# Attention and two gated layers on one core: a second handoff time in the planner, output products held four parts behind, and one attention's due times moved

## The chip, the cores and the metric

The kernel runs on one core of a Trainium2 chip. The metric is the device time of one execution in microseconds (us), the median over several executions. The engines are TensorE (PE in the profile; its weight loads are PEld), VectorE (DVE), ScalarE (ACT), GpSimd (POOL) and SyncE (SP), which issues all the transfers here.

## The reference

Everything is float32. The reference is three steps in a row over 4608 tokens of 512 features:

```python
scores = scale * (q_c @ k_c.T)            # chunks of 64 tokens, 8 heads of 64
attn = exp(scores - max) / (sum + 1e-9)
x = (attn @ v_c)                          # -> 4608 x 512
g = x @ w_gate                            # first layer, 512 -> 1536 -> 512
x = (g * sigmoid(g) * (x @ w_val)) @ w_out
h = x @ w_in                              # second layer, 512 -> 2048 -> 512
out = (h * sigmoid(1.702 * h)) @ w_out2
```

## The kernel before, in words

**Tiling.** The tokens are cut into nine blocks of 512. The first layer's 12 feature tiles are done in two passes over all blocks (six tiles a pass, three groups of two), the second layer's 16 in two more passes (eight tiles a pass, two groups of four). So pass 0 and 1 are the first layer, pass 2 and 3 the second, and a second-layer pass has nine blocks of two groups. Sums between the two passes of a layer go through DRAM (`y_dram`, `o_dram`). The last pass adds the kept sum and writes `out`.

**Products.** Every matrix product is done as seven half-size products (labels 1 to 7) with sums of quarters before and after, and every operand is split into a high and a low part, so that one product is 12 matmuls of 256 columns (`mm3`, L247 to L250: high by high, high by low, low by high). A second-layer group has seven input products (`product`, L567) and then 14 output parts (`last_product`, L713: two for each of seven labels, six matmuls each).

**The shared bank.** In `group_gated` (L631) the seven input products of a group are written into one PSUM bank, `ga`, one after the other in the order 1, 6, 7, 5, 2, 4, 3 (only the very first second-layer group gives three of them banks of their own). Each product must wait until the previous one's reader has read the bank. These readers stand in `follow` (L659): an ACT copy for labels 1, 6, 7 and 5, and a DVE addition for 2, 4 and 3. Behind the readers comes the chain that makes the operands of the output parts: a sigmoid on ACT and a product on DVE (`gate`, L646), sums on DVE, and the split into a high part (a cast on ACT) and a low part (a subtraction on DVE or POOL) in `parts` (L655). While a reader runs, TensorE does output parts of an earlier group.

**The order.** No engine's order is written out by hand. Every operation is recorded with an engine, an estimated duration, a priority (a due time; the lower comes first) and its dependencies; `Program.emit` (L99) then walks a model of the engines: it takes on each engine the operation that could start first, and of those that could start within 0.3 us of it (0.1 us on DVE) the one of the lowest priority. This order is the order of the engine's queue, which is processed in order on the chip. The model's time from the end of one operation to the start of one that needs it is `late`: 0.3 us between engines, 1.2 us into TensorE, 1.5 us more after a transfer, 0.13 us on the same engine. The input products of the second layer are marked `near` and get 0.25 us. The model has no contention between engines.

**Due times.** In the main loop (L864 on) the output parts of a group wait in a list, `pend`. After each of the next group's seven products, `put` takes some of them off the list, records them, and gives them the due time of that point; in the second layer two after each product, until none is left after the seventh. The order of the labels is 1, 2, 4, 5, 6, 7, 3. `o_sum` (L731), called with the second part of a label in a block's second group, adds the outputs up: in the last pass it loads the sum of the earlier pass (`part_of`), adds to it on POOL and DVE, and stores to `out` (`out_quarter`).

**The start.** In pass 0 the attention of the next block (four calls of `attend`, L463, of 128 tokens each) is recorded with each block. Each has loads of q, k and v (issued by SP, due 10 us ahead), two sets of 32 small matmuls and a transposition on TensorE, six DVE operations (L487 to L495), an exponential and two copies on ACT. `x_made` (L538) then makes the seven input operands of the block (sums on DVE, casts on ACT, subtractions on POOL). Next to this the first layer's weights are unpacked and split on ACT, DVE and POOL (`conv_part`, `split`).

Of the kernel before, what the change touches and what calls it, by code (L numbers as in the profile page):

```python
# [69 lines left out]
class Program:  # L70


    def __init__(self):
        self.ops = []

    def op(self, eng, us, fn, reads=(), writes=(), prio=0, table=None, near=False):
        o = Op()
        o.eng, o.us, o.fn, o.prio, o.table, o.near, o.n = eng, us, fn, prio, table, near, len(self.ops)
        deps, follows = set(), set()
        for b in reads:  # L80
            deps.update(next((a.writers for a in b.line() if a.writers), ()))
        for b in writes:
            deps.update(b.users)
            if not b.users:
                if b.prev is not None:
                    deps.update(b.prev.users)
                if b.before is not None and b.before.tile is None:
                    follows.add(b.before.users[0])
        for b in (*reads, *writes):
            for a in b.line():  # L90
                a.users.append(o)
        for b in writes:
            for a in b.line():
                a.writers.append(o)
        o.deps, o.follows = deps, follows - deps
        self.ops.append(o)
        return o

    def emit(self):  # L99
        waiting = {o: len(o.deps) + len(o.follows) for o in self.ops}  # L100
        after = {}
        for o in self.ops:
            for d in (*o.deps, *o.follows):
                after.setdefault(d, []).append(o)
        ready = {}
        for o in self.ops:
            o.done_at = 0.0
            if not waiting[o]:
                ready.setdefault(o.eng, []).append(o)
        free, table = {}, None  # L110
        left = len(self.ops)
        while left:
            pick = None
            for eng, todo in ready.items():
                if not todo:
                    continue
                t = free.get(eng, 0.0)
                start = [max(t, o.done_at) for o in todo]
                first = min(start)
                s, o = min(((s, o) for s, o in zip(start, todo) if s <= first + (0.1 if eng == "dve" else 0.3)), key=lambda x: (x[1].prio, x[1].n))  # L120
                if pick is None or s < pick[0]:
                    pick = s, o
            s, o = pick
            ready[o.eng].remove(o)
            free[o.eng] = s + o.us + (1.3 if o.table and o.table != table else 0.0)
            end = free[o.eng] + (2.0 if o.eng == "dma" else 0.0)
            table = o.table or table
            o.fn()
            left -= 1
            for a in after.get(o, ()):  # L130
                if o in a.deps:
                    late = (0.3, 1.2)[a.eng == "pe" and o.eng != "pe"] + (1.5 if o.eng == "dma" else 0.0)
                    if a.near and o.eng != "dma":
                        late = 0.25
                    a.done_at = max(a.done_at, end + ((0.0 if a.eng == "pe" else 0.13) if a.eng == o.eng else late))
                waiting[a] -= 1
                if not waiting[a]:
                    ready.setdefault(a.eng, []).append(a)
# [3 lines left out]
def attention_two_moe_kernel(ctx: ExitStack, tc: tile.TileContext, q, k, v, wg, wv, wo, wi, wo2, out):  # L142
# [38 lines left out]
    UPB = BT // P  # L181
    EARLY = 8
    FILL = 24
    scale = 1.0 / float(D) ** 0.5

    pool = {}
# [25 lines left out]
    def act_us(n):  # L212
        return (200 + n) / 1.2e3
# [13 lines left out]
    def store(dst, src, writes, prio):  # L227
        op("dma", 0.74 / 512 * size(dst), lambda: nc.sync.dma_start(out=dst, in_=bits(src.ap)), [src], writes, prio)

    def copy(dst, src, n, prio, eng="act", cut=lambda ap: ap):  # L230
        if eng == "act":
            op("act", act_us(n), lambda: nc.scalar.copy(out=dst.ap, in_=cut(src.ap)), [src], [dst], prio)  # L232
        elif eng == "pool":
            op("pool", pool_us(0.6 * n), lambda: nc.gpsimd.tensor_copy(dst.ap, cut(src.ap)), [src], [dst], prio)  # L234
        else:
            op("dve", dve_us(n), lambda: nc.vector.tensor_copy(dst.ap, cut(src.ap)), [src], [dst], prio)

    def tt(dst, a, b, by, n, prio, eng="dve", of_a=lambda ap: ap, of_b=lambda ap: ap):
        e = nc.vector if eng == "dve" else nc.gpsimd
        op(eng, dve_us(n) if eng == "dve" else pool_us(n),  # L240
           lambda: e.tensor_tensor(out=dst.ap, in0=of_a(a.ap), in1=of_b(b.ap), op=by), [a, b], [dst], prio)  # L241

    def split(hi, lo, src, n, prio, eng="dve", cut=lambda ap: ap, hi_eng="act"):
        copy(hi, src, n, prio, hi_eng, cut)
# [319 lines left out]

    n_groups = [0]

    def product(m, w, x, goes_on, prio, near=False):  # L567

        def fn():
            for var in range(2):  # L570
                for kk in range(2):
                    ks = slice(kk * P, kk * P + P)
                    mm3(m.ap[:, var], w.ap[:, var, 0, ks], w.ap[:, var, 1, ks], x.ap[:, 0, kk], x.ap[:, 1, kk],
                        kk == var == 0 and not goes_on, kk == 1, skip_group_check=True)

        op("pe", GV, fn, [w, x], [m], prio, near=near)
# [54 lines left out]
    def group_gated(g, xs, at, put, early):  # L631
# [27 lines left out]
        def follow(label, prio):  # L659
            m = bank[label]  # L660
            if label == "1":
                copy(s1, m, 512, prio)
            elif label == "6":
                copy(u2, m, 512, prio)
            elif label == "7":
                copy(u3, m, 512, prio)
                tt(u2, u2, u3, ALU.subtract, 512, prio, "pool")
            elif label == "5":
                c = quarter()
                copy(c, m, 512, prio)  # L670
                tt(u2, u2, c, ALU.add, 512, prio, "pool")
                a["22"] = gate(c, 3, prio + 1)
                parts("4", a["22"], prio + 3, "pool")
            elif label == "2":
                c = quarter()
                tt(c, s1, m, ALU.add, 512, prio)
                a["11"] = gate(c, 0, prio + 1)
                parts("1", a["11"], prio + 2)
            elif label == "4":
                c = quarter()  # L680
                tt(c, u3, m, ALU.subtract, 512, prio)
                a["12"] = gate(c, 1, prio + 1)
                parts("2", a["12"], prio + 3)
            else:
                c = quarter()
                tt(c, u2, m, ALU.add, 512, prio)
                a["21"] = gate(c, 2, prio + 1)

        a = {}
# [2 lines left out]
        bank = {label: ring[alone[label]].new([P, 2, HT]) if label in alone else z for label in ORDER[2]}  # L692
        for i, label in enumerate("1263745" if early else ORDER[2]):
            n = ORDER[2].index(label)
            product(bank[label], W[g][n], xs[n], label in "675", at(i), True)
            if label != "3" or not early:
                follow(label, at(i))
            if i == 6:
# [32 lines left out]
    def o_sum(p, b, label, banks, kept, prio):  # L731
# [31 lines left out]
        elif label == "6":  # L763
            tt(kept["s"], kept["s"], m, ALU.add, 512, prio)
        elif label == "7":
            u2, u3 = kept["s"], ring["e"].new([P, 2, 256])
            tt(u3, u2, m, ALU.add, 512, prio)
            c = part_of(3, "yv")
            if final:
                tt(c, c, u3, ALU.add, 512, prio, "pool")  # L770
                tt(c, c, banks["5"], ALU.add, 512, prio)
            else:
                tt(c, u3, banks["5"], ALU.add, 512, prio)
            out_quarter(3, c)
            tt(u3, u3, banks["4"], ALU.subtract, 512, prio)
            if final:
                c = part_of(2, "t")
                tt(c, c, u3, ALU.add, 512, prio, "pool")
                u3 = c
            out_quarter(2, u3)  # L780
            tt(u2, u2, banks["5"], ALU.add, 512, prio)
        elif label == "3":
            u4 = kept["s"]
            tt(u4, u4, m, ALU.add, 512, prio)
            if final:
                c = part_of(1, "t")
                tt(c, c, u4, ALU.add, 512, prio, "pool")
                u4 = c
            out_quarter(1, u4)

    y_dram = pool["dram"].tile([P, KD, NT], F32, name="y_dram")
# [72 lines left out]
    for p, (layer, gs) in enumerate(passes):  # L864
        jobs = spread(p)
        for b in range(NB):
            t = start[p][b]
            xs = X.pop((p, b))
            for j, g in enumerate(gs):
# [3 lines left out]
                after_first = p and passes[p - 1][0] < layer and b == j == 0  # L873

                def put(i, tj=tj, n=n, step=step, layer=layer, after_first=after_first):
                    left = n * (7 - i - (i > 3)) // 8 if layer == 1 else 0 if after_first else n * (6 - i) // 7
                    while len(pend) > left:
                        pend.pop(0)(tj + (i + (i > 4) + 0.5 + (n - len(pend) if after_first else 0)) * step / 8)

# [3 lines left out]
                if layer == 1:  # L883
# [4 lines left out]
                    for n, (m, hh, hl) in enumerate(gated(g, c, tj + step)):  # L888
                        for e in range(KD):
# [9 lines left out]

                            pend.append(fn)  # L900
                else:
                    parts = group_gated(g, xs, at, put, after_first)
                    if j == 0:
                        banks, kept = {}, {}
# [25 lines left out]
                end = j == len(gs) - 1  # L930
                if p == 0 and b + 1 < NB:
                    for u in range(UPB * j // len(gs), UPB * (j + 1) // len(gs)):
                        at = t - 22 + u * 14
                        attend(UPB * (b + 1) + u, at, at - 10)
                    if end:
                        x_made(b + 1, start[p][b + 1] - 20)
# [53 lines left out]
```

## Time and profile before

| what | us |
|---|---|
| median of 3 runs | 1806.77 |
| lowest and highest | 1804.65, 1808.59 |
| the profiled execution | 1805.41 |
| its span, first to last instruction | 1803.6 |

The profiled execution is 1.4 us under the median. Its span lies 1.8 us below its own time. Busy time in the span: TensorE's matmuls 1718.8 us (95%), VectorE 1302.3 (72%), ScalarE 883.6 (49%), GpSimd 751.5 (42%). The granted TensorE clock averages 0.987 of full speed. A matmul's time in the trace overlaps the next one's, so the number of matmuls in a stretch tells more than the busy share. The stretches: pass 0 with attention from 0 to about 570 us, pass 1 to about 1030, pass 2 to about 1434, pass 3 to the end.

### The profile page before, as it was taken

What the parts mean: (1) busy time and instruction counts of PE and PEld (TensorE: products, weight loads), DVE (VectorE), ACT (ScalarE), POOL (GpSimd) and SP (SyncE); (2) the same over time, 40 slices, a digit from 0 to 9 for tenths busy, and PEclk for the clock granted to TensorE, in tenths of its full rate; (3) what the DMA queues carried; (4) which work ended last, traced back from release to release, by engine and by line L of the source; (5) the groups of instructions that cost most, each with busy time, mean ns of one, the idle gap of its engine ahead of it and who ended that gap; (6) DMA issues with size and microseconds to landing.
All of it is one profiled execution on the core that took longest, in us unless ns stands there. A gap on an engine that the chain in (4) does not pass through costs nothing.

```text
span 1803.6 us, 36622 instructions
## 1 busy us (share of the span) xinstructions
PE 1718.8 (95%) x14392; PEld 1623.1 (90%) x14392; DVE 1302.3 (72%) x1884; ACT 883.6 (49%) x1536; POOL 751.5 (42%) x762
## 2 busy tenths in 40 slices
PE   7779999999999999999999979999999999999997
PEld 6769988989899999999999878999999999999997
DVE  6887878778875576655555589899776677777676
ACT  5766665666663344333333355555444444444443
POOL 5665455445651254322222256676411233333333
PEclk8989999999999999999999989999999999999999
DMA  6468887788769988877779988888768976677764
GB/s 257 172 215 280 271 282 239 251 292 292 241 234 360 323 300 304 293 252 245 243 244 327 371 307 295 287 295 299 252 223 295 356 238 224 221 223 226 227 212 133
DMA packets 187324, 477.92 MB, mean 265 GB/s; under 512 B 20112, under 2 KB 47760, under 8 KB 187152
## 3 DMA queue, kind: packets, MB, share of 16 engines
q1 hardware_dynamic: 187152, 475.58, 77.6%
q8 instruction: 114, 1.87, 0.4%
q14 instruction: 58, 0.48, 0.1%
HBM read 334.46 MB, written 141.03 MB: 264 GB/s over the span
## 4 chain that ended last, share of the span: by engine, by line
PE 72%; DVE 14%; issue 3%; ACT 3%; DMA 2%; POOL 1%; SPq 0%; POOLq 0%; DVEq 0%; ACTq 0%
PE ga L248 9%; PE ga L250 8%; PE ga L249 8%; DVE xr L241 4%; PE yb L248 4%; PE gb L248 4%; PE yb L250 4%; PE yb L249 4%; PE gb L250 4%; PE gb L249 4%; PE ya L249 3%; PE ya L248 3%; PE ya L250 3%; PE s L248 2%; PE s L250 2%
## 5 line engine op out<-in xcount | busy, mean ns | idle before, releaser
L248 PE MATMUL ga<-x,w 128*128 128x256 f32 x1652 | 480.1, 291 | 44.3 <-ACT u L232 29.7
L250 PE MATMUL ga<-x,w 128*128 128x256 f32 x1652 | 468.2, 283 | 1.0 <-POOL w L241 1.0
L249 PE MATMUL ga<-x,w 128*128 128x256 f32 x1652 | 467.4, 283 | 0.0
L248 PEld LDWEIGHTS ga<-x,w 128*128 128x128 f32 x1652 | 313.8, 190 | 65.3 <-ACT u L232 37.9
L249 PEld LDWEIGHTS ga<-x,w 128*128 128x128 f32 x1652 | 314.0, 190 | 4.1
L250 PEld LDWEIGHTS ga<-x,w 128*128 128x128 f32 x1652 | 313.9, 190 | 1.5 <-POOL w L241 1.5
L232 ACT COPY u<-ga 128x512 f32<-128x512 f32 x231 | 135.2, 585 | 177.2 <-PE ga L250 172.6
L241 DVE TENSOR_TENSOR xr<-xr,c 128x512 f32<-128x512 f32 x144 | 129.6, 902 | 103.9 <-ACT xr L650 99.8
L241 DVE TENSOR_TENSOR h<-h,c 128x512 f32<-128x512 f32 x216 | 167.6, 792 | 12.6 <-ACT h L612 10.9
L241 DVE TENSOR_TENSOR c<-u,ga 128x512 f32<-128x512 f32 x146 | 99.9, 684 | 68.0 <-PE ga L250 66.2
L248 PE MATMUL gb<-x,w 128*128 128x256 f32 x496 | 143.0, 288 | 1.1 <-DVE c L241 1.1
L249 PE MATMUL gb<-x,w 128*128 128x256 f32 x496 | 141.4, 285 | 1.1 <-POOL x L241 1.1
L250 PE MATMUL gb<-x,w 128*128 128x256 f32 x496 | 141.7, 286 | 0.0
L241 POOL TENSOR_TENSOR u<-u 128x512 f32<-128x512 f32 x36 | 48.0, 1333 | 197.7 <-ACT u L232 197.5
L612 ACT ACTIVATE h<-c 128x512 f32<-128x512 f32 x108 | 68.2, 633 | 121.1 <-DVE c L241 120.7
L241 DVE TENSOR_TENSOR c<-u,gb 128x512 f32<-128x512 f32 x124 | 84.5, 682 | 57.2 <-ACT u L232 35.4
L232 ACT CAST hh<-xr 128x512 fp32r<-128x512 f32 x108 | 66.8, 620 | 116.8 <-DVE xr L241 116.8
L241 DVE TENSOR_TENSOR xr<-xr 128x512 f32<-128x512 f32 x144 | 118.9, 825 | 4.2 <-POOL hl L241 0.6
L650 ACT ACTIVATE xr<-c 128x512 f32<-128x512 f32 x144 | 90.7, 632 | 58.3 <-DVE c L241 52.7
L234 POOL CAST ws<-t 128x256 fp32r<-128x256 f32 x78 | 46.1, 591 | 164.0 <-DMA od_b<-ws 83.6
L241 POOL TENSOR_TENSOR k<-xr,q 128x512 fp32r<-128x512 f32 x24 | 41.4, 1724 | 156.6 <-DVE xt L241 89.4
L248 PEld LDWEIGHTS gb<-x,w 128*128 128x128 f32 x496 | 95.3, 192 | 4.2 <-DVE c L241 1.3
(237 smaller groups left out, 5125.1 us busy)
## 6 DMA issues: line engine op xcount, KB each, us to landing
x<-x_dram SPq DMA_DIRECT2D x189, 512.0 KB, 5.2
o<-od_b SPq DMA_DIRECT2D x126, 512.0 KB, 4.3
o<-od_a SPq DMA_DIRECT2D x102, 512.0 KB, 5.1
x_dram<-x SPq DMA_DIRECT2D x63, 512.0 KB, 4.7
wd_b<-ws SPq DMA_DIRECT2D x56, 256.0 KB, 4.7
od_b<-ws SPq DMA_DIRECT2D x56, 256.0 KB, 4.4
w<-wd_b SPq DMA_DIRECT2D x28, 512.0 KB, 6.6
raw<-in_moe_w_out SPq DMA_DIRECT2D x56, 255.8 KB, 4.7
```

What stands on the lines that cost most here:

```text
L232: op("act", act_us(n), lambda: nc.scalar.copy(out=dst.ap, in_=cut(src.ap)), [src], [dst], prio)
L234: op("pool", pool_us(0.6 * n), lambda: nc.gpsimd.tensor_copy(dst.ap, cut(src.ap)), [src], [dst], prio)
L241: lambda: e.tensor_tensor(out=dst.ap, in0=of_a(a.ap), in1=of_b(b.ap), op=by), [a, b], [dst], prio)
L248: nc.tensor.matmul(o, ah, bh, start=first, stop=False, **kind)
L249: nc.tensor.matmul(o, ah, bl, start=False, stop=False, **kind)
L250: nc.tensor.matmul(o, al, bh, start=False, stop=last, **kind)
L612: op("act", act_us(512), lambda h=h, i=i: nc.scalar.activation(out=h.ap, in_=of(0)(c[i].ap), func=AF.Sigmoid), [c[i]], [h], prio, "sig")
L650: op("act", act_us(512), lambda: nc.scalar.activation(out=h.ap, in_=c.ap, func=AF.Sigmoid, scale=1.702), [c], [h], prio, "sig")
```

## The change

`Program` gets a field `slack`, None at first and set to 1.0 when the first second-layer group is recorded (it stays so). An operation recorded without a `near` of its own on ACT, DVE or POOL takes `slack` as its `near`. `near` is now a time and no longer a mark: where it is set, it is the model's handoff time between engines in place of 0.3 us (not after a transfer, and not on the same engine). So from there on these operations have 1.0 us; the readers of the shared bank get 0.3 us and the input products 0.25 us, both as before. TensorE's output parts keep 1.2 us.

In `put`, the second layer's rule leaves at least four output parts (two labels) on the list: a group's parts are recorded two products later, with due times two products later. In `o_sum` the two last quarters are added in another order; in the last pass, POOL adds the kept sum for the last quarter ahead of the last product and DVE adds the last product's bank after it. The due times of block 1's four attention calls, recorded with block 0 of pass 0, go from -22, -8, 6, 20 to 4, 20, 36, 52, and those of their loads with them. No operation is added or left out.

```diff
-    def op(self, eng, us, fn, reads=(), writes=(), prio=0, table=None, near=False):
+    def op(self, eng, us, fn, reads=(), writes=(), prio=0, table=None, near=None):
         o = Op()
-        ... = eng, us, fn, prio, table, near, len(self.ops)
+        ... = eng, us, fn, prio, table, self.slack if near is None and eng not in ('pe', 'dma') else near, len(self.ops)
...
-                    if a.near and o.eng != "dma":
-                        late = 0.25
+                    if a.near is not None and o.eng != "dma":
+                        late = a.near
...
+    LAG = 4
...
             if label == "1":
-                copy(s1, m, 512, prio)
+                copy(s1, m, 512, prio, near=0.3)
...
             elif label == "2":
                 c = quarter()
-                tt(c, s1, m, ALU.add, 512, prio)
+                tt(c, s1, m, ALU.add, 512, prio, near=0.3)
...
-            product(bank[label], W[g][n], xs[n], label in "675", at(i), True)
+            product(bank[label], W[g][n], xs[n], label in "675", at(i), 0.25)
...
             out_quarter(3, c)
-            tt(u3, u3, banks["4"], ALU.subtract, 512, prio)
+            c = part_of(2, "t") if final else u3
             if final:
-                c = part_of(2, "t")
                 tt(c, c, u3, ALU.add, 512, prio, "pool")
-                u3 = c
-            out_quarter(2, u3)
             tt(u2, u2, banks["5"], ALU.add, 512, prio)
+            tt(c, c, banks["4"], ALU.subtract, 512, prio)
+            out_quarter(2, c)
+            if final:
+                kept["c"] = part_of(1, "t")
+                tt(kept["c"], kept["c"], u2, ALU.add, 512, prio, "pool")
         elif label == "3":
-            u4 = kept["s"]
+            u4 = kept["c" if final else "s"]
             tt(u4, u4, m, ALU.add, 512, prio)
-            if final:
-                c = part_of(1, "t")
-                tt(c, c, u4, ALU.add, 512, prio, "pool")
-                u4 = c
             out_quarter(1, u4)
...
-                    left = n * (7 - i - (i > 3)) // 8 if layer == 1 else 0 if after_first else n * (6 - i) // 7
+                    left = n * (7 - i - (i > 3)) // 8 if layer == 1 else 0 if after_first else max(LAG, n - 2 * i - 2)
...
                 else:
+                    prog.slack = 1.0
                     parts = group_gated(g, xs, at, put, after_first)
...
-                        at = t - 22 + u * 14
+                        at = t - 22 + u * 14 if b else t + 4 + u * 16
                         attend(UPB * (b + 1) + u, at, at - 10)
```

The readers of labels 6, 7, 5, 4 and 3 get `near=0.3` in the same way, and `copy` and `tt` hand it on.

## Rows read from the trace of the kernel before

**Rows 1.** the page, busy time of TensorE, share of the span, instructions

```profile
PE 1718.8 (95%) x14392; PEld 1623.1 (90%) x14392; DVE 1302.3 (72%) x1884; ACT 883.6 (49%) x1536; POOL 751.5 (42%) x762
```

**Rows 2.** busy time by stretch: length, then PE, PEld, DVE, ACT, POOL (instructions), clock, DMA

```profile
38.00:128.00 90.00, 68.95 (x677) 60.69 (x678) 78.28 (x113) 63.38 (x124) 65.28 (x65) 0.89 0.54 191
1026.00:1076.00 50.00, 37.61 (x260) 34.46 (x260) 39.73 (x55) 26.84 (x50) 23.87 (x22) 0.93 0.93 333
1100.00:1300.00 200.00, 191.49 (x1560) 187.81 (x1559) 174.25 (x232) 105.59 (x189) 132.72 (x146) 0.99 0.87 288
1300.00:1384.00 84.00, 83.69 (x695) 82.69 (x695) 58.07 (x87) 38.33 (x64) 15.62 (x13) 1.00 0.70 231
1475.00:1727.00 252.00, 245.36 (x2017) 240.85 (x2016) 180.29 (x247) 109.89 (x187) 82.38 (x60) 1.00 0.72 226
```

**Rows 3.** who waited for whom, pass 3 (1434 to 1768): total, times, longest

```profile
PE ga L248 <- ACT u L232: 7.2, 15, 0.6
...
PEld ga L248 <- DVE c L241: 2.8, 8, 0.3
```

**Rows 4.** instructions in order of time, ACT, one place in pass 3: start, length

```profile
1600.55 0.62 ACT L232 CAST v<-xr 128x512 fp32r<-128x512 f32 x1 [1.08 <-DVE xr L241]
1601.28 0.62 ACT L232 CAST q<-xr 128x512 fp32r<-128x512 f32 x1
1601.81 0.58 ACT L232 COPY u<-ga 128x512 f32<-128x512 f32 x1
```

**Rows 5.** the same place on DVE and POOL

```profile
1597.64 3.61 DVE L241 TENSOR_TENSOR xr<-xr 128x512 f32<-128x512 f32 x3
...
1596.59 3.37 POOL L241 TENSOR_TENSOR t<-t,e 128x512 f32<-128x512 f32 x2 [2.03 <-DVE e L241]
```

**Rows 6.** groups of instructions by form, pass 3: busy, mean ns, idle before

```profile
L241 DVE TENSOR_TENSOR xr<-xr 128x512 f32<-128x512 f32 x63 | 55.2, 876 | 1.9
L241 DVE TENSOR_TENSOR c<-u,ga 128x512 f32<-128x512 f32 x48 | 33.0, 688 | 18.9 <-PE ga L250 17.8
...
L232 ACT COPY u<-ga 128x512 f32<-128x512 f32 x47 | 27.5, 585 | 20.9 <-PE ga L250 20.9
...
L241 POOL TENSOR_TENSOR t<-t,e 128x512 f32<-128x512 f32 x16 | 27.0, 1708 | 16.2 <-DVE e L241 16.2
L241 POOL TENSOR_TENSOR u<-u 128x512 f32<-128x512 f32 x16 | 20.8, 1298 | 77.7 <-ACT u L232 77.7
```

**Rows 7.** who PE waited for, 1100 to 1300 us (pass 2 beside weight preparation)

```profile
PE ga L248 <- ACT u L232: 4.9, 4, 2.2
PE ga L248 <- DVE c L241: 3.4, 8, 0.7
```

**Rows 8.** who PE waited for, 1026 to 1076 us (from first to second layer)

```profile
PE ga L248 <- ACT u L232: 5.2, 5, 1.9
```

**Rows 9.** DVE groups by form, 38 to 128 us: three of an attention's six operations

```profile
L495 DVE TENSOR_TENSOR e<-e,z 128x512 f32<-128x512 f32 x6 | 5.0, 841 | 0.1
L487 DVE TENSOR_REDUCE m<-s 128x8 f32<-128x512 f32 x7 | 4.7, 677 | 0.0
L492 DVE TENSOR_SCALAR z<-z 128x8 f32<-128x8 f32 x6 | 4.7, 785 | 0.1
```

**Rows 10.** who PE waited for, 26 to 130 us

```profile
PE a L506 <- DVE e L495: 6.7, 2, 4.1
```

**Rows 11.** instructions in order of time, POOL: the last of block 1's x

```profile
124.94 1.47 POOL L241 TENSOR_TENSOR x<-xr,x 128x512 fp32r<-128x512 f32 x1
```

**Rows 12.** the end, in order of time: DVE, POOL and the transfers' issue

```profile
1797.99 0.69 DVE L241 TENSOR_TENSOR e<-e,a 128x512 f32<-128x512 f32 x1
...
1795.41 1.27 POOL L241 TENSOR_TENSOR yv<-yv,e 128x512 f32<-128x512 f32 x1 [8.28 <-DVE e L241]
1798.09 2.48 POOL L241 TENSOR_TENSOR t<-t,e 128x512 f32<-128x512 f32 x2 [1.40 <-DVE e L241]
...
1799.38 1.59 SPq L228 DMA_DIRECT2D out<-t  x2
```

More of the change, by code (lines that the diff above doesn't have):

```diff
@@ L73, in __init__ @@
     def __init__(self):
-        self.ops = []
-    def op(self, eng, us, fn, reads=(), writes=(), prio=0, table=None, near=False):
+        self.ops, self.slack = [], None
+    def op(self, eng, us, fn, reads=(), writes=(), prio=0, table=None, near=None):
         o = Op()
-        o.eng, o.us, o.fn, o.prio, o.table, o.near, o.n = eng, us, fn, prio, table, near, len(self.ops)
+        o.eng, o.us, o.fn, o.prio, o.table, o.near, o.n = eng, us, fn, prio, table, self.slack if near is None and eng not in ('pe', 'dma') else near, len(self.ops)
         deps, follows = set(), set()
@@ L228, in store, with copy @@
         op("dma", 0.74 / 512 * size(dst), lambda: nc.sync.dma_start(out=dst, in_=bits(src.ap)), [src], writes, prio)
-    def copy(dst, src, n, prio, eng="act", cut=lambda ap: ap):
+    def copy(dst, src, n, prio, eng="act", cut=lambda ap: ap, near=None):
         if eng == "act":
-            op("act", act_us(n), lambda: nc.scalar.copy(out=dst.ap, in_=cut(src.ap)), [src], [dst], prio)
+            op("act", act_us(n), lambda: nc.scalar.copy(out=dst.ap, in_=cut(src.ap)), [src], [dst], prio, near=near)
         elif eng == "pool":
@@ L236, in copy, with tt @@
             op("dve", dve_us(n), lambda: nc.vector.tensor_copy(dst.ap, cut(src.ap)), [src], [dst], prio)
-    def tt(dst, a, b, by, n, prio, eng="dve", of_a=lambda ap: ap, of_b=lambda ap: ap):
+    def tt(dst, a, b, by, n, prio, eng="dve", of_a=lambda ap: ap, of_b=lambda ap: ap, near=None):
         e = nc.vector if eng == "dve" else nc.gpsimd
         op(eng, dve_us(n) if eng == "dve" else pool_us(n),
-           lambda: e.tensor_tensor(out=dst.ap, in0=of_a(a.ap), in1=of_b(b.ap), op=by), [a, b], [dst], prio)
+           lambda: e.tensor_tensor(out=dst.ap, in0=of_a(a.ap), in1=of_b(b.ap), op=by), [a, b], [dst], prio, near=near)
     def split(hi, lo, src, n, prio, eng="dve", cut=lambda ap: ap, hi_eng="act"):
@@ L565, in attention_two_moe_kernel, with product @@
     n_groups = [0]
-    def product(m, w, x, goes_on, prio, near=False):
+    def product(m, w, x, goes_on, prio, near=None):
         def fn():
@@ L661, in follow @@
             if label == "1":
-                copy(s1, m, 512, prio)
+                copy(s1, m, 512, prio, near=0.3)
             elif label == "6":
-                copy(u2, m, 512, prio)
+                copy(u2, m, 512, prio, near=0.3)
             elif label == "7":
-                copy(u3, m, 512, prio)
+                copy(u3, m, 512, prio, near=0.3)
                 tt(u2, u2, u3, ALU.subtract, 512, prio, "pool")
@@ L669, in follow @@
                 c = quarter()
-                copy(c, m, 512, prio)
+                copy(c, m, 512, prio, near=0.3)
                 tt(u2, u2, c, ALU.add, 512, prio, "pool")
@@ L680, in follow @@
                 c = quarter()
-                tt(c, u3, m, ALU.subtract, 512, prio)
+                tt(c, u3, m, ALU.subtract, 512, prio, near=0.3)
                 a["12"] = gate(c, 1, prio + 1)
@@ L685, in follow @@
                 c = quarter()
-                tt(c, u2, m, ALU.add, 512, prio)
+                tt(c, u2, m, ALU.add, 512, prio, near=0.3)
                 a["21"] = gate(c, 2, prio + 1)
```

## The prediction

> **What bounds the kernel.** I read the page first: TensorE's matmuls cover 95% of the span [rows 1]. So the time is TensorE's work plus the holes in it, and a change of order can win holes alone. Where they are is read from the table by stretch, by counting matmuls. Late in pass 2, when no weights are prepared any more, 84 us hold 695 matmuls, 8.27 in a us [rows 2]. A second-layer block has 336 (two groups of 84 for the input products and 84 for the output parts), so an undisturbed block takes 40.6 us. In pass 3, 252 us hold 2017, 8.00 in a us, and a block takes 42.0. In pass 2 beside the weight preparation it is 1560 in 200 us, 7.80 in a us. At the start, from 38 to 128 us, TensorE is busy for 69 of 90 us while VectorE is busy for 78.
>
> What makes a hole in pass 3 is in the list of waits: nearly all of TensorE's is on ACT's copy `u`, 7.2 us in 15 waits, two in a block; the DVE addition `c`, a reader too, holds up the weight load for 2.8 us in 8 [rows 3]. One such place in order of time shows why [rows 4]. The copy `u` frees the shared bank and starts at 1601.81. In ACT's queue it stands behind two casts of the chain. The first of them waited 1.08 us for DVE, with ACT idle. DVE was late because three subtractions took 3.61 us in all; POOL was at work on two additions of the last pass at that time [rows 5]. So the cause is not load (ACT is busy for 44% of pass 3 [rows 2]) but a place in a queue: the model expected the cast to be ready earlier than it was.
>
> **The readers in front.** Nothing is added or removed; the model now takes 1.0 us instead of 0.3 us from engine to engine for everything but the readers and TensorE's operations. In each four-hop stretch (sigmoid, product, cast, subtraction) the chain comes 4 x 0.7 = 2.8 us later in the model, so more readers are placed ahead of chain operations that they used to follow. The gain where it works fully: pass 3 falls to the undisturbed rate, 42.0 - 40.6, unrounded 1.35 us a block, for eight blocks (the ninth runs into the tail) 10.8 us. The least is nothing, if other operations come to stand in front. I take 10.8: two waits of one kind in each block have one cause, and it is the one that the edit is about. The DVE readers' waits (2.8 us) I leave where they are; they are the upper end.
>
> Pass 2 beside weight preparation falls short of the undisturbed rate by 200 x 8.27 - 1560 = 94 matmuls, 11.4 us. The waits there are 4.9 us on `u` and 3.4 us on `c` [rows 7]. The weights' own operations get 1.0 us as well, and they are many, so I take only the 4.9 us on the copies, as 5; bounds 0 and 11.4.
>
> Between the layers, 5.2 us of TensorE's waits are on `u` [rows 8]. But the first group has no older output parts to fill holes with, and its chain, now placed later, is what TensorE waits for next. I take 1 us of gain, bounds -3 and 5.
>
> **The output parts four behind.** This costs no instruction. A chain operation that moves behind a reader is late by that reader, 0.585 us [rows 6], and TensorE's output parts wait for it. What covers it: a part is six matmuls, at 8.27 a us 0.73 us, and four of them are 2.9 us, just over the 2.8 us that the chain is put back. If the cover is gone, the price is a rival below. SP's loads of the output weights move with the due times; they are due 14 us before their part, as before. By itself I put this at 0: TensorE takes whichever part is ready when a reader runs, and the due time only decides between ready ones.
>
> **The sums at the end.** Before, after the last product's bank, DVE adds (0.69 us from 1797.99), then POOL does two additions, 2.48 us together, and the last store is issued in the stretch from 1799.38 to 1800.97 [rows 12]. After the change DVE alone stands between bank and store. But POOL's three additions now follow each other from 1795.41 on: 1.27 + 2.48 = 3.75 us, to 1799.2, and DVE's 0.69 us after that gives about 1799.9 where the second POOL addition ended at 1800.6. Gain 0.6 us; bounds 0 and 1.9 (both POOL hops gone, 2.48 less the handoffs). In the other blocks of the pass the stores are waited for by no one.
>
> **Block 1's attention.** Three of its six DVE operations are 0.84, 0.68 and 0.79 us [rows 9]; with two more like the second and a short one it is some 3.8 us each, an estimate. Today parts of the attention stand in DVE's queue in front of block 0's first operands and readers, and TensorE waits 6.7 us for `e` in two places [rows 10]. Moved back, the first products come earlier. But DVE is busy for 87% from 38 to 128 us [rows 2], the work must still be done, and block 1 can't begin before its operands: POOL's last ends at 126.4 [rows 11]. SP's loads of q, k, v come later and free the queue for the weights at first. Bounds: a gain of 6.7 us; a loss of 10.3 us if block 1's seven POOL subtractions (1.47 us each [rows 11]) come wholly behind block 0. I take a gain of 3, under half of the waits on `e`.
>
> **The sum.** 10.8 + 5 + 1 + 0.6 + 3 = 20.4 us. The profiled execution took 1805.4 us, so 1785.0 for it; it lies 1.4 us under the median of the runs, so the forecast is **1786 us**. A measurement of this kernel can tell about 0.2% (3.6 us) from no change.
>
> **Rivals.** (a) *Readers in front help, the rest does not*: only the 10.8 us of pass 3 less a third where a DVE reader takes the copy's place, and nothing at the start: 7 us, 1800 us. For it: due times decide only between ready operations. Against it: both waits of a block have the same picture.
>
> (b) *Block 1 starts late*: the layer's gain of 16.8 and 0.6 us stays, the start loses 10.3: 7.1 us of gain, also 1800. For it: the last of the four calls is due at 52, after all of block 0's products, and block 2's attention can't overtake it (one buffer each). Against it: these operations come as soon as their engine is free, whatever their due time.
>
> (c) *The holes move but stay.* The late operation in rows 5 is late because of POOL. Rows of pass 3 show this throughout: DVE's subtractions with two SBUF operands average 876 ns, the readers with one PSUM operand 688 ns; POOL's addition beside them takes 1708 ns where another of its size takes 1298 [rows 6]. The model knows nothing of that, and no handoff constant follows it; the same 63 subtractions meet the same POOL additions at another place, and another copy waits. Gain nothing: 1807 us. The Trainium skill ("SBUF — State Buffer", Who interferes with whom) says that DVE and GpSimd share a port pair under an exclusive lock, held for a whole instruction, which a DVE operation takes if it has two SBUF inputs; by that rule the lost time belongs to the pair of operations and not to the order of the copies, which is this rival. The rows agree on which operations are stretched.
>
> (d) *Slower: the chain runs out of cover.* If the chain grows by more than the 2.9 us of four output parts, TensorE stands still before a part in every group. The price of one reader's copy, 0.585 us, in each of 36 groups (two passes, nine blocks, two groups) is 21 us; less 3.6 for start and end, 1805.4 + 17.5 + 1.4 = 1824 us. For it: 2.8 against 2.9 is narrow. Against it: the real handoffs are far below the model's (ACT's cast of `q` starts at 1601.28, DVE's third subtraction ends at 1597.64 + 3.61 = 1601.25 [rows 4, 5]), and a hole, once taken, leaves more parts in reserve.
>
> **Chances.** Forecast 0.45, (a) 0.11, (b) 0.09, (c) 0.15, (d) 0.20. Faster by over 0.2% are the forecast, (a) and (b): 0.65; within 0.2% (c): 0.15; slower (d): 0.20. Range: at the low end the forecast with the other bounds, 2.8 us for the DVE readers, 6.4 more in pass 2, 3.7 more at the start, rounded 1773. At the high end it goes past no change into (d) up to 1814, where the cover fails in a third of the groups (7 us). Left out are most of (d), some 0.15, and 0.05 below. The likeliest case alone: 1777 to 1797.
>
> **What would show it.** Right: in pass 3 the waits on ACT's `u` are nearly gone and a 252 us stretch holds some 2080 matmuls; in ACT's order of time `u` stands in front of the casts of `v` and `q`; in the stretch from 1100 to 1300 us the waits on `u` fall below 2 us; the last store is issued less than 2 us after the last bank's DVE addition. Wrong: TensorE waiting for `hl`, `h`, `k` or `xt` before `ya`, `yb`, `gb` or `s` in every group (d), as many waits on `u` as before at other labels (c), or block 1's last operand on POOL later than 126 us (b).

## The result and the profile after

After the change the kernel takes 1790.5 us (median of 4 runs, 1790.05 to 1794.59) against 1807.5 before (median of 4, the 3 runs shown and one more): 0.9913 of the time, 95% interval 0.9895 to 0.9932, so 0.9% less. The forecast was 1786 us in a range of 1773 to 1814, faster. The size and the sign were right. The reasons were in good part not: the runs below give the gain to another part of the change than the forecast did, and show that two parts of it cost time. That the total came out near the forecast is therefore in good part luck.

The table by stretch, columns as in [rows 2], of the kernel after:

```profile
38.00:128.00 90.00, 68.72 (x674) 60.69 (x675) 78.77 (x115) 62.88 (x122) 63.92 (x63) 0.85 0.56 196
1026.00:1076.00 50.00, 38.00 (x279) 35.57 (x278) 36.62 (x47) 24.39 (x46) 23.96 (x22) 0.97 0.86 312
1100.00:1300.00 200.00, 196.09 (x1631) 194.18 (x1631) 175.69 (x245) 109.28 (x198) 125.05 (x135) 1.00 0.85 287
1300.00:1384.00 84.00, 83.93 (x706) 83.72 (x706) 62.07 (x92) 38.13 (x65) 29.20 (x27) 1.00 0.82 286
1475.00:1727.00 252.00, 248.40 (x2065) 245.96 (x2064) 191.53 (x254) 112.63 (x191) 89.62 (x61) 1.00 0.71 233
```

The start holds as many matmuls as before (674 for 677 in 90 us). Pass 2 beside the weight preparation has 1631 in 200 us for 1560; late pass 2, which I had taken for undisturbed, 706 in 84 us for 695; pass 3 has 2065 in 252 us for 2017. Along the trace, the start of a given matmul (counted from 0) shows where the time went. The 8400th (end of the first layer) starts at 1024.4 us for 1023.8 before: nothing won, and the 0.6 us say nothing, since the ten runs below that have the first layer of before reach it from 1022.0 to 1027.0 us. From the 8400th to the 8800th, between the layers, the change takes 74.1 us for 71.0, a loss. The 9200th starts at 1146.8 for 1148.0, the 11600th (early in pass 3) at 1438.0 for 1445.0, the 14000th at 1731.2 for 1745.2, and the span ends at 1788.5 for 1803.6. So of 15.1 us, 7.0 came up to matmul 11600 and 7.1 from there to matmul 14000, in pass 3; the last 1.1 came after it.

Who TensorE waited for after the change, in pass 3 (1425 to 1755 us); the whole list is one line:

```profile
PE yb L249 <- DVE t L242: 3.5, 7, 0.5
```

And from 1100 to 1300 us, again one line:

```profile
PE ga L249 <- DVE c L242: 3.5, 4, 1.5
```

The waits on ACT's `u` [rows 3, 7] are gone in both. But pass 3 has a new one, seven times in 330 us: an output part, into bank `yb`, waits for DVE's `t`. One such place in order of time (start, length, idle before), ACT first:

```profile
1667.34 0.59 ACT L233 COPY u<-ga 128x512 f32<-128x512 f32 x1 [2.32 <-PE ga L251]
1667.83 0.62 ACT L233 CAST h<-xr 128x512 fp32r<-128x512 f32 x1
1668.35 0.62 ACT L233 CAST v<-xr 128x512 fp32r<-128x512 f32 x1
1670.19 0.58 ACT L233 COPY u<-ga 128x512 f32<-128x512 f32 x1 [1.23 <-PE ga L251]
1670.68 0.62 ACT L233 CAST q<-xr 128x512 fp32r<-128x512 f32 x1
```

DVE at the same place:

```profile
1668.79 1.76 DVE L242 TENSOR_TENSOR h<-xr,h 128x512 fp32r<-128x512 f32 x1
1670.47 1.77 DVE L242 TENSOR_TENSOR xr<-xr 128x512 f32<-128x512 f32 x1
1672.17 1.77 DVE L242 TENSOR_TENSOR xt<-xr,v 128x512 fp32r<-128x512 f32 x1
1673.87 0.68 DVE L242 TENSOR_TENSOR yv<-yv,yb 128x512 f32<-128x512 f32 x1
1674.47 1.18 DVE L242 TENSOR_TENSOR k<-xr,q 128x512 fp32r<-128x512 f32 x1
1675.57 0.68 DVE L242 TENSOR_TENSOR t<-t,yb 128x512 f32<-128x512 f32 x1
1676.17 0.68 DVE L242 TENSOR_TENSOR xt<-xr,xt 128x512 fp32r<-128x512 f32 x1
...
1677.37 0.68 DVE L242 TENSOR_TENSOR c<-u,ga 128x512 f32<-128x512 f32 x1
```

POOL at the same place:

```profile
1668.28 3.43 POOL L242 TENSOR_TENSOR t<-t,e 128x512 f32<-128x512 f32 x2
1671.66 1.74 POOL L242 TENSOR_TENSOR u<-u 128x512 f32<-128x512 f32 x1
1673.73 1.37 POOL L242 TENSOR_TENSOR u<-u,c 128x512 f32<-128x512 f32 x1 [0.33 <-ACT c L233]
```

ACT's copies now start when TensorE has finished, no longer behind a late cast. DVE is the late engine: three operations of 1.76 us on two operands in SBUF, beside POOL's two additions and a subtraction, and later `t<-t,yb`, the subtraction that the change put behind POOL's addition and that frees `yb`, and then the reader `c`. The Trainium skill ("SBUF — State Buffer", Who interferes with whom) says that a DVE instruction with two SBUF inputs contends with a GpSimd instruction that reads SBUF. The trace agrees: the 1.76 us are of that kind, `xt<-xr,xt` takes 0.68 us once POOL is done, and `yv<-yv,yb`, which reads one operand from a PSUM bank, takes 0.68 us beside POOL's `u<-u,c`.

### The profile page after: what moved, and what is told of

Read it like the earlier page. It is cut to its first block, busy times and chain, and to the rows that moved or that the text cites. A ratio compares the mean times of both kernels' runs of the same rounds, so it can differ in the third digit from the quotient of the medians.

```text
span 1788.5 us, 36703 instructions
## 1 busy us (share of the span) xinstructions
PE 1711.5 (96%) x14392; PEld 1623.6 (91%) x14392; DVE 1310.8 (73%) x1884; ACT 876.9 (49%) x1534; POOL 761.6 (43%) x762
## 4 chain that ended last, share of the span: by engine, by line
PE 75%; DVE 15%; issue 3%; DMA 1%; ACT 1%; POOL 0%; POOLq 0%; SPq 0%; DVEq 0%; ACTq 0%
PE ga L249 9%; PE ga L251 9%; PE ga L250 9%; PE yb L249 4%; PE ya L250 4%; PE ya L251 4%; PE ya L249 4%; PE yb L251 4%; PE yb L250 4%; PE gb L249 4%; PE gb L251 4%; PE gb L250 4%; DVE xr L242 3%; PE s L249 2%; PE s L251 2%
## 5 line engine op out<-in xcount | busy, mean ns | idle before, releaser
L242 POOL TENSOR_TENSOR u<-u 128x512 f32<-128x512 f32 x36 | 53.7, 1492 | 191.7 <-ACT u L233 191.7
L242 DVE TENSOR_TENSOR xr<-xr,c 128x512 f32<-128x512 f32 x144 | 115.7, 809 | 14.2 <-ACT xr L651 14.2
L235 POOL CAST ws<-st 128x256 fp32r<-128x256 f32 x88 | 48.4, 549 | 121.2 <-DMA od_b<-ws 54.0
```

## The experiments

All runs were timed against the kernel before on the same chip, and ratios are to its runs there. Held-back parts means `LAG = 4`; handoff times means the field `slack` with the readers' 0.3 us.

**1. Handoff times alone**

```diff
-                    left = ... max(LAG, n - 2 * i - 2)
+                    left = ... n * (6 - i) // 7
```

and the sums and the attention's due times as before.

> Only the handoff times (1.0 us, readers 0.3 us) are taken over; output parts, sums and attention as before. Theory A (the readers' place in the queues is the gain): most of the second layer's gain of 14 us comes, 1793 to 1798 us, and in pass 3 the waits on ACT's u fall from 7.2 us to under 1. Theory B (the chain put back needs the four parts as cover): TensorE waits for hl, h or xt before the output parts, and the time is 1805 us or more.

Measured: 1809.0 us, ratio 1.0025 (1.0012 to 1.0038), slightly slower. Its table by stretch, columns as in [rows 2]:

```profile
1100.00:1300.00 200.00, 188.06 (x1513) 182.91 (x1513) 171.53 (x231) 104.24 (x188) 130.43 (x145) 0.99 0.85 285
1300.00:1384.00 84.00, 82.17 (x674) 80.38 (x672) 54.59 (x83) 36.65 (x63) 15.59 (x12) 1.00 0.65 207
1475.00:1727.00 252.00, 251.38 (x2079) 247.92 (x2079) 187.44 (x257) 112.47 (x191) 86.61 (x63) 1.00 0.72 232
```

Pass 3 gains what was forecast for it: 2079 matmuls for 2017, and no wait on `u`. Pass 2 loses: 1513 for 1560 and 674 for 695. In the list from 1100 to 1300 us there are now output parts that wait for the chain:

```profile
PE ga L249 <- ACT u L233: 5.9, 6, 1.9
PE ga L249 <- DVE c L242: 3.3, 6, 0.9
PE ya L251 <- DVE hl L242: 2.5, 4, 0.7
```

So theory A holds in pass 3 and fails in pass 2, where the waits on `u` have not gone (4.9 us before). B holds there in part: the waits on `hl` are 2.5 us and `u` has 1.0 us more, and the rest of the 47 matmuls, nearly 6 us, does not stand in the list.

**2. Held-back parts alone**

```diff
-                    left = ... n * (6 - i) // 7
+                    left = ... max(LAG, n - 2 * i - 2)
```

on the kernel before, nothing else.

> Only the four output parts are held back; handoff times, sums and attention as before. Theory A: the copies u stay behind the casts, so the waits of 7.2 us in pass 3 stay and the time is within 4 us of 1807. Theory C (the reserve of parts fills the holes, whatever the order of the readers): 1793 to 1798 us.

Measured: 1777.2 us, ratio 0.9850 (0.9837 to 0.9864). The part that I had put at 0 gives 1.5%, more than the whole change. Its table by stretch:

```profile
1100.00:1300.00 200.00, 196.68 (x1633) 194.78 (x1634) 177.81 (x251) 112.38 (x199) 121.08 (x129) 1.00 0.85 290
1300.00:1384.00 84.00, 83.95 (x702) 83.41 (x702) 59.62 (x84) 38.21 (x65) 29.93 (x29) 1.00 0.82 276
1475.00:1727.00 252.00, 252.00 (x2109) 250.82 (x2108) 181.03 (x256) 116.80 (x197) 87.12 (x63) 1.00 0.72 231
```

Pass 2 is as in after, pass 3 far better, and TensorE's list of waits in pass 3 is empty. As the whole reason, theory A falls.

**3. Both, with the sums and the attention as before**

> Handoff times and held-back parts together, sums and attention as before. From the trace of after: start +0.7 and sums about 7 us lost in pass 3 against 1.5 us won at the end. If that reading holds, this is faster than after by some 5 us: 1785 us, without the wait of yb on DVE's t in pass 3. If the wait on yb has another cause than the new sums, 1790 to 1793 us.

Measured: 1781.0 us, ratio 0.9867 (0.9852 to 0.9882): faster than after, by more than expected, with 2124 matmuls in pass 3's 252 us and no wait. But it is 4 us over the second run, with the handoff times as the only difference. They lose around the change of layer: between the 8400th and the 8800th matmul this run takes 8.0 us more than the second. In its list from 1026 to 1100 us one reader is waited for 5.5 us, and one output part waits 3.7 us for DVE's `h`:

```profile
PE ga L249 <- DVE c L242: 8.2, 4, 5.5
PE yb L251 <- DVE h L242: 3.7, 1, 3.7
```

DVE there, in order of time:

```profile
1040.51 1.75 DVE L242 TENSOR_TENSOR e<-xr,t 128x512 fp32r<-128x512 f32 x1
1043.01 2.50 DVE L242 TENSOR_TENSOR xr<-xr,c 128x512 f32<-128x512 f32 x4 [0.76 <-ACT xr L651]
1045.43 0.68 DVE L242 TENSOR_TENSOR c<-u,ga 128x512 f32<-128x512 f32 x1
```

And ACT there:

```profile
1042.35 2.19 ACT L651 ACTIVATE xr<-c 128x512 f32<-128x512 f32 x4 [3.86 <-DVE e L242]
```

The sigmoids write the one `xr` buffer, so they waited 3.86 us until DVE had read the last first-layer block out of it (`e<-xr,t`, the last operand made from it). DVE's four products wait for the sigmoids, and the reader `c`, ready long before, stands behind them. Here the longer handoff times did the reverse of their purpose.

**4. The attention's due times alone**

> Only the due times of block 1's attention are moved. By the traces (matmul number 8000 comes 0.7 us later after than before): within 2 us of before, 1805 to 1809 us. As forecast: 3 us faster, 1804 us.

Measured: 1807.1 us, ratio 1.0010 (0.9999 to 1.0022). No gain; the upper end is a loss of 4 us. From 38 to 128 us it has 676 matmuls for 677.

**5. After, with the sums put back**

> After, with the order of the sums put back; handoff times, held-back parts and attention as after. If the new sums are what makes TensorE wait 0.65 + 0.26 us in each block of pass 3 (yb for DVE's t, then ga for DVE's c), those waits go, DVE's xr from xr falls from 883 to about 750 ns, and the time is 8 us less in pass 3, 1 us more at the end: 1783 us. If they come from the moved attention or from nothing of this: 1790 us.

Measured: 1784.3 us, ratio 0.9878 (0.9864 to 0.9891), as expected. Pass 3 has 2122 matmuls in 252 us for 2065 with the new sums, TensorE's list there is empty, and DVE's group by form (busy, mean ns) falls from 883 ns to

```profile
L242 DVE TENSOR_TENSOR xr<-xr 128x512 f32<-128x512 f32 x52 | 38.8, 746 | 0.7
```

At 8.42 matmuls in a us the 57 are 6.8 us in six blocks, 9 us in eight: what the new sums cost. At the end they win: from the last matmul's start to the end of the span it is 4.5 us in after, 5.6 here.

**6. Only the sums' operations later.** The second run left two readings: the reserve of parts on TensorE, or the sums, whose due times hang on those of the parts.

```diff
-                                    o_sum(p, b, label, banks, kept, prio + 0.5)
+                                    o_sum(p, b, label, banks, kept, prio + 5.5)
```

on the kernel before.

> Before, with one thing changed: the operations of the output sums are due 5 us (two products) later; output parts are not held back. Theory S (holding the parts back helps because the sums' additions on POOL and DVE get out of the chain's way): DVE's xr from xr falls from 869 towards 750 ns in pass 3, the waits on ACT's u go, 1792 to 1798 us. Theory R (what helps is the reserve of output parts on TensorE): 1803 to 1808 us, waits on u as before.

Measured: 1785.8 us, ratio 0.9884 (0.9871 to 0.9898), a larger gain than theory S was expected to give. No output part is held back, and pass 3 has the same 2109 matmuls as the second run, with an empty list of waits. Two lines of its table by stretch:

```profile
1100.00:1300.00 200.00, 192.15 (x1593) 189.71 (x1592) 175.57 (x242) 107.29 (x191) 134.11 (x145) 1.00 0.89 291
...
1475.00:1727.00 252.00, 251.88 (x2109) 250.65 (x2108) 190.06 (x259) 116.19 (x196) 82.53 (x61) 1.00 0.74 234
```

The chain's subtraction is no longer stretched, as the groups by form show (1475 to 1727 us; busy, mean ns). Before:

```profile
L241 DVE TENSOR_TENSOR xr<-xr 128x512 f32<-128x512 f32 x49 | 42.6, 869 | 1.5
L241 DVE TENSOR_TENSOR xt<-xr,xt 128x512 fp32r<-128x512 f32 x12 | 8.3, 692 | 4.7 <-ACT xt L232 4.1
```

In this run:

```profile
L242 DVE TENSOR_TENSOR xr<-xr 128x512 f32<-128x512 f32 x51 | 34.9, 685 | 1.6 <-DVE xr L242 0.5
L242 DVE TENSOR_TENSOR xt<-xr,xt 128x512 fp32r<-128x512 f32 x12 | 12.2, 1020 | 4.4 <-ACT xt L233 4.4
```

The second line of each pair shows that the stretch has not gone but moved, to operations that make TensorE wait nowhere in pass 3. DVE's busy time for one instruction in this stretch is 0.73 us in both runs (180.29 / 247 [rows 2] and 190.06 / 259). The readers' handoff times are as before, and at the place of [rows 4] the copy still stands behind the casts. But the casts now come in time, and it waits for TensorE alone:

```profile
1604.05 0.62 ACT L233 CAST v<-xr 128x512 fp32r<-128x512 f32 x1
1604.63 0.62 ACT L233 CAST q<-xr 128x512 fp32r<-128x512 f32 x1
1605.95 0.59 ACT L233 COPY u<-ga 128x512 f32<-128x512 f32 x1 [0.69 <-PE ga L251]
```

In pass 3 theory S is the whole answer. The edit moves the sums on DVE and those on POOL at once, so which of the two stood more in the way is not shown. Beside the weight preparation it is half: 1593, between 1560 and 1633.

**7. Two behind**

```diff
-    LAG = 4
+    LAG = 2
```

on the second run's kernel.

> As the run with held-back parts alone, but two parts instead of four. Theory R: about half of the 28 us, 1790 to 1795 us. Theory S: one product's time is enough to let the chain pass ahead of the sums or it is not, so either near 1777 or near 1805 us, with DVE's xr from xr showing which.

Measured: 1783.2 us, ratio 0.9866 (0.9850 to 0.9882). Pass 3 again has 2109 matmuls and 685 ns for the subtraction; from 1100 to 1300 us it is 1585. The time lies between the two that theory S allowed and below the one of theory R. In pass 3, one product's time is enough to get the sums out of the chain's way. Beside the weight preparation two parts do no more than the sums alone (1593 in the sixth run), and four do (1633). So theory S holds in pass 3, and beside the weight preparation the parts themselves count too; through which wait was not followed.

**8. Four behind, new sums in the last block only**

```diff
+            if final and b == NB - 1:
...
+                tt(kept["c"], kept["c"], u2, ALU.add, 512, prio, "pool")
+                return
```

> Held-back parts alone, and the new order of the sums in the very last block only. The end after the last matmul gets shorter by what it is in after (from 5.9 to 4.4 us), nothing else changes: 1 to 1.5 us under the held-back parts alone, 1776 us. If the new sums hold yb up at the end as well: 1777 us or more.

Measured: 1776.4 us, ratio 0.9829 (0.9813 to 0.9846). The stretch after the last matmul's start is 4.3 us for 5.5 in the second run, as expected; in the total that cannot be told from the scatter. Apart from the last two instructions on DVE, its order of instructions on TensorE, ACT, DVE and POOL is that of the second run, yet from 1100 to 1300 us it has 1621 matmuls for 1633: differences of that size say nothing.

**9. Both, but the handoff times not in the first second-layer block**

```diff
-                    prog.slack = 1.0
+                    prog.slack = 1.0 if b or p == NPASS - 1 else None
```

on the third run's kernel.

> Handoff times and held-back parts as in the third run, but in pass 2 the handoff time of 1.0 us is set only from block 1 on. In the third run the stretch around the change of layer (matmuls 8400 to 8800) took 8 us more than with held-back parts alone, with TensorE waiting 5.5 us for one DVE reader. If the cause is that the readers of the first group stand behind chain operations that wait for a buffer, 5 to 8 us come back: 1773 to 1776 us, and no wait over 3 us on DVE's c between 1026 and 1100 us. If the cause is the handoff time of the weight preparation: 1780 us as before.

Measured: 1774.9 us, ratio 0.9826 (0.9811 to 0.9842). The longest wait on DVE's `c` around the change of layer falls from 5.5 to 2.5 us, the wait on `h` is gone, and from the 8400th to the 8800th matmul 7.1 of the 8.0 us come back. The reader now stands in front on DVE:

```profile
1044.82 0.67 DVE L242 TENSOR_TENSOR c<-u,ga 128x512 f32<-128x512 f32 x1
1045.41 1.16 DVE L242 TENSOR_TENSOR e<-xr,t 128x512 fp32r<-128x512 f32 x1
```

The rest of the weight preparation has the handoff times as well, and loses nothing by them: it holds 1648 matmuls for the second run's 1633 (table by stretch):

```profile
1100.00:1300.00 200.00, 197.62 (x1648) 196.19 (x1647) 179.24 (x251) 110.32 (x201) 123.86 (x134) 1.00 0.85 289
```

**10. Handoff times in pass 3 only, on the eighth run's kernel**

> Held-back parts, the new sums in the last block, and the handoff time of 1.0 us in pass 3 alone. From the third run's pass 3 (2124 matmuls in 252 us against 2109 with held-back parts alone: 0.3 us a block): 2 to 2.5 us under the run with the new sums in the last block, 1774 us. If the handoff times cost something at the end: 1776 us.

Measured: 1776.0 us, ratio 0.9832 (0.9817 to 0.9847). Pass 3 has 2123 matmuls for 2110, as expected, but 6.6 us follow the last matmul's start instead of 4.3. Of the two outcomes expected it is the second, 1776 us with something lost at the end; from the eighth run the time cannot be told apart.

**11. Eight behind, on the eighth run's kernel**

> Eight parts held back instead of four, new sums in the last block. If the reserve counts (theory R), pass 2 beside the weight preparation gains further, 1772 to 1774 us. If it is the place of the sums (theory S), four is enough and the sums come into the chain's way again at another place or the operands' buffers are held too long: 1777 us or more.

Measured: 1781.5 us, ratio 0.9859 (0.9841 to 0.9876). From 1100 to 1300 us there are 1596 matmuls, fewer than the 1621 of the eighth run. More reserve does not help (ratio 0.9859 for the eighth run's 0.9829); what stands in the way then was not followed.

**12. Together: the ninth run with the new sums in the last block only**

> The ninth run (handoff times from block 1 of pass 2 on, four parts held back, attention as before) with the new sums in the last block only. If the parts add: the end after the last matmul falls from 5.5 to about 4.3 us and the time is 1 us under the ninth run, 1774 us. If the order at the end shifts with the handoff times, as in the tenth run (6.6 us after the last matmul), no gain: 1775 us.

Measured: 1772.5 us, ratio 0.9822 (0.9808 to 0.9835): faster than both given kernels. The end after the last matmul's start is 4.5 us for 5.5 in the ninth run, as expected. Its interval overlaps those of runs 8, 9 and 10, so the last step is not shown apart in the total. Its table by stretch:

```profile
1100.00:1300.00 200.00, 197.61 (x1648) 196.25 (x1647) 179.32 (x251) 112.50 (x203) 123.11 (x132) 1.00 0.85 290
1300.00:1384.00 84.00, 84.00 (x710) 84.00 (x709) 61.33 (x87) 38.26 (x65) 29.65 (x28) 1.00 0.84 292
1475.00:1727.00 252.00, 252.00 (x2124) 252.00 (x2123) 185.58 (x255) 115.66 (x197) 88.73 (x64) 1.00 0.72 231
```

2124 in 252 us are 8.43 in a us: late pass 2 and pass 3 then run without a hole that a profile shows (TensorE busy for 84.00 of 84 and 252.00 of 252 us); beside the weight preparation 2.4 of 200 us are left.

## Why the prediction was right, and where it was not

**What bounds the kernel** held: only holes on TensorE could be won, and they went where the text had found them. "Undisturbed" was too low a mark: 8.27 matmuls in a us became 8.43.

**Readers in front, 10.8 + 5 + 1 us.** In pass 3 the mechanism and the size were right for this edit alone: the waits on `u` go, and (2079 - 2017) / 8.25 = 7.5 us in six blocks, 10 in eight. The step that failed is giving 5 us in pass 2 to the readers. The stretch did win 71 matmuls in the whole change, some 8.6 us and within the stated bounds, but the held-back parts alone win 73 there (run 2), and the handoff times alone lose 47 from 1100 to 1300 us, nearly 6 us, and 21 more by 1384 us (run 1). That is in part rival (d): without the four parts, output parts wait for `hl`; with them, none does in the list of after. "I take 1 us of gain" between the layers failed too: the change loses 3.1 us there, the handoff times cost 8 us against the held-back parts alone (runs 3 and 2), and run 9 shows that this comes from the first second-layer block, where a reader is placed behind products that wait for a buffer.

**The output parts four behind, 0 us.** This is the main failure: alone they gain 28 us. The sentence "TensorE takes whichever part is ready when a reader runs, and the due time only decides between ready ones" is about TensorE. I put the edit at nothing by an argument about one engine, and left out that the output sums take their due times from the parts, and that on DVE and POOL several operations are ready at once. I had the row for it: the three subtractions that took 3.61 us beside POOL's additions [rows 5]. Those additions are output sums, and moving them is what this edit does (run 6). Beside the weight preparation part of the gain needs the parts themselves to be later (runs 2, 6, 7); why is open.

**The sums at the end, 0.6 us.** The end is 1.5 us shorter (6.0 to 4.5 us after the last matmul's start). The step that failed is "in the other blocks of the pass the stores are waited for by no one". The stores are not, but the bank that the subtraction frees is. Putting the sums back takes away its wait and the stretch of the chain's subtraction together, 9 us in eight blocks (run 5).

**The attention, 3 us.** Measured between 0 and 4 us of loss. The step that failed is counting the waits on `e` [rows 10] as a gain: in run 4 they fall from 6.7 to 4.1 us, but waits on `hl` and `hh`, 1.0 and 1.3 us before, take their place, and DVE is busy for 88% of the stretch after 87. From its list, 26 to 130 us:

```profile
PE ya L250 <- DVE hl L242: 4.3, 2, 3.1
PE a L507 <- DVE e L496: 4.1, 1, 4.1
PE ya L249 <- ACT hh L233: 3.9, 2, 3.5
```

**The sum.** 20.4 us were forecast, 15.1 came in the profiled runs. With the second run as the base it reads: held-back parts -28, handoff times on top +4, the rest +8 to 9 (sums and attention), most of it the sums (run 5 against after). A term put at 0 won more than the whole, and others that were counted as gains lost: that they came to nearly the forecast is luck. Of the rivals, (c) named the right conflict, POOL against DVE, and was right that the stretch stays and only moves. It was wrong that another copy must then wait: due times move the stretch off the three subtractions in front of the casts (run 6), and so do the handoff times in pass 3 (691 ns in run 1).

**The signs.** Nearly all signs of being right came: no waits on `u`, copies in front of the casts, a last store issued within 2 us of the last bank's addition, 2065 matmuls for "some 2080". They did not tell the forecast's cause from another: in run 6 the waits on `u` go too, with the readers' handoff times as before.

## What to carry to other kernels

Where a hole ends on a reader, look at what made the engine in front of it late before reordering the reader: here the cause was work that nobody waits for soon (output sums), given a due time too early, in the way of work that TensorE needs (in pass 3 the whole cause, beside the weight preparation a part). When a due time is moved, list everything that inherits it, on every engine, and look for the queue on which several of these are ready at once. A change of several edits is worth taking apart even where it wins: one of these four gave more than all together, and one of the others paid only outside the first block.

## What the runs showed of the hardware that was not expected

Operations with two SBUF operands on DVE and operations on POOL that meet stretch each other: three in a row on DVE at 1.76 us beside POOL's at 1.7 us, where apart they take 0.69 us (run 6) and 1.30 us [rows 6]. The stretch stands inside both records and not as idle time. It does not add up to a loss for the pair. Meeting, the starts of DVE's operations are 1.7 us apart (1668.79, 1670.47, 1672.17). Apart, DVE's starts are 0.60 us apart (1675.57, 1676.17) and two additions on POOL take 2.48 us [rows 12], so one of each, one after the other, needs 0.60 + 1.24 = 1.84 us. What is lost is time on DVE, where a short operation that TensorE needs lasts as long as the long one on POOL that nobody needs soon.

Another order need not remove the stretch. In the fastest run, `k<-xr,q` takes 1000 ns in pass 3 where it takes 681 before, and TensorE has no hole there. What counts is which operations are stretched.
